# One-core attention and Strassen-type layer on Trainium2: running sums of phase one kept in PSUM, alpha folded into the weights, attention steps placed anew, early loads for phase two

## The chip, the cores and the metric

The kernel runs on one core of one Trainium2 chip. A core has TensorE (PE), VectorE (DVE), ScalarE (ACT), GpSimd (POOL) and SyncE (SP), which here only issues DMAs. The metric is the time of one execution on the device in microseconds. The kernel before has a median of 1134.48 us over 3 runs (1133.36 to 1135.65).

## The reference

All data are float32: 8 batches, 8 heads, 576 positions, head size 64; 4608 tokens of width 512; 2048 hidden features.

```python
k_p = k.reshape(B, H, 72, 8, D).mean(axis=3)      # v_p in the same way
scores = scale * q @ k_p.T;  scores -= max;  attn = exp(scores)
attn = attn / (attn.sum(-1) + 1e-09)
x = (attn @ v_p), heads side by side               # 4608 x 512
h = x @ w_in                                       # 4608 x 2048
g = h + sin(alpha * h)**2 / (alpha + 1e-09)        # alpha: one number per hidden feature
out = g @ w_out                                    # 4608 x 512
```

## The kernel before

**Tiling.** The tokens are cut into nine units of 512. Phase one makes x, h and g of unit after unit and stores g to a buffer in DRAM (`g_bridge`); phase two loads g and multiplies by `w_out`. Both matrix products are done by a Strassen-Winograd scheme: each factor is a 2 x 2 array of blocks, and seven block products with sums of blocks as operands take the place of eight.

**Phase one.** `hidden(u)` (L210 to L266) forms four sums of the blocks of x on VectorE (L210), then goes through four weight groups J = 0 to 3. A group is seven products of eight matmuls of 256 columns each (L222), in the order 1, 6, 7, 5, 2, 4, 3, into banks of the PSUM pool `ps_m` (five banks; the attention has three others, `ps_a`). Product 1 is copied to SBUF by ScalarE (`p1`), VectorE adds products 6 and 7 to it (`u2`, `u3`, L227 and the lines after it) and gets the four blocks of h from these sums; product 2 is added by the matmuls themselves onto the bank of product 1, and product 4 onto that of product 7. Then ScalarE takes four sines (L259) with alpha as the scale and one square over all 2048 columns (L260), VectorE adds the squares times 1/(alpha + 1e-9) to h (L264, four instructions), and SP stores the megabyte (L266).

**Attention.** `attention(b)` is a generator. One step is the transposes of pooled keys (L89), of queries, a score pair with its maximum (VectorE), the two exponentials of all tiles at once (L121), the norm of one tile (two VectorE operations and the reciprocal, then a multiply on POOL, L130), transposes of weights (L139), values (L153) or a rest. For batch 0 all steps run in the head, one after the other. While unit u computes, two steps of batch u + 1 are taken after each product, until they are used up. `load_batch` (L60 to L74) issues the loads of a batch and pools keys and values by eight on POOL (keys of batch 0 on VectorE).

**Weights.** `load_w_in` (L175 to L184) loads eight pieces of 512 KB on SP and forms three sums and differences per group and a fourth block, 16 instructions in all, on POOL (L179); ScalarE negates `a22`. `load_w_out` (L194, L195) is called at unit 7, after attention's pools have been closed: four loads of a megabyte into their memory, and four differences of 2048 elements on POOL.

**Phase two.** `output(u)` (L276 to L323) loads four megabytes of g in five buffers shared with the four sums per group that VectorE forms (`gs`, L279), and does seven products of 16 matmuls (L292) in the order 1, 6, 2, 7, 5, 4, 3. The pool of these buffers is opened only when the pools of phase one are closed.

**Order.** The instructions are written in one stream; a tile scheduler fixes each engine's order by its own estimate of times, adds the semaphores, and gives memory out. Each engine works through its queue in order, and so does SP with its DMAs.

In the program's names `a` are blocks of `w_in` and `as` sums of them, `b` and `bt` the same of `w_out` (`bt` also the sums of x), `ex` the exponentials, `ral` is 1/(alpha + 1e-9), `s` holds sines and squares.

## Time and profile before

| | |
|---|---|
| median of 3 runs | 1134.48 us |
| the profiled execution: its time, its span | 1131.5 us, 1129.7 us |
| mean granted TensorE clock over the span | 0.963 |
| PE, DVE, ACT, POOL busy | 92%, 50%, 26%, 22% of the span |
| head, first matmul of unit 0 | until 50.2 us |
| phase one ends, phase two starts | 670.8 us, 687.0 us |
| DMA over the span | 122.48 MB, mean 108 GB/s |

The span runs from the first to the last instruction that the hardware recorded. A group row gives line, engine, operation, output<-inputs, shape and count, then busy time and mean ns, then the idle time of the engine just ahead of these instructions and what ended most of it. A timeline row gives start and length in us, and in brackets the wait ahead of it and who ended it. A row of a stage gives start and end, length, busy time and count of each engine, the granted clock (1.00 is full), the share of the DMA engines and GB/s. A row of digits shows tenths in 40 equal slices. PE's busy time is modelled, so gaps between starts say more than it does.

### The profile page before, as it was taken

The numbers are of one execution on the slowest core, as the hardware profiler recorded it, in microseconds if no ns is written. First come the engines' busy times: TensorE is split into PE (matmuls) and PEld (weight loads), VectorE is DVE, ScalarE is ACT, GpSimd is POOL, SyncE is SP. The second block draws the span as 40 slices with busy tenths as digits, with TensorE's granted clock in tenths as the row PEclk, the third lists the DMA queues.
The fourth block names the chain that finished last, engine by engine and source line by source line (L and its number), as shares of the span: only waits on it lengthen the run. The fifth ranks groups of instructions, "written<-read, shape, count | busy, mean of one in ns | idle before, by whom it ended". The sixth has DMA issues, their size and how long they took to land. (4 is left out here: it accounts for less than half of the span.)

```text
span 1129.7 us, 13110 instructions
## 1 busy us (share of the span) xinstructions
PE 1041.6 (92%) x5248; PEld 880.1 (78%) x5248; DVE 565.4 (50%) x1019; ACT 296.2 (26%) x386; POOL 245.9 (22%) x248
## 2 busy tenths in 40 slices
PE   4579999989899899999949976999999999999998
PEld 3367777868778688888838865888888888888887
DVE  5548685785857667577674554033140413314030
ACT  2234444454443544445423540000000000000000
POOL 4997571350714502102060000000000000000000
PEclk9689999999999899999979997999999999999999
DMA  7363450612605214111242115134050432505120
GB/s 195 117 168 116 140 177 38 180 68 83 184 38 158 81 75 128 61 52 75 77 147 112 75 74 223 60 127 157 30 186 5 182 109 78 186 1 187 59 91 37
DMA packets 71212, 122.48 MB, mean 108 GB/s; under 512 B 41968, under 2 KB 46064, under 8 KB 61936
## 3 DMA queue, kind: packets, MB, share of 16 engines
q1 hardware_dynamic: 71152, 121.66, 31.7%
q8 instruction: 41, 0.67, 0.2%
q14 instruction: 19, 0.16, 0.0%
HBM read 74.46 MB, written 47.19 MB: 108 GB/s over the span
## 5 line engine op out<-in xcount | busy, mean ns | idle before, releaser
L222 PE MATMUL ps_m<-bt,a 128*128 128x256 f32 x576 | 143.6, 388 | 19.5 <-DVE u L227 19.5
L292 PE MATMUL ps_m<-b,g 128*128 128x256 f32 x576 | 131.0, 383 | 16.1 <-issue 16.1
L222 PE MATMUL ps_m<-bt,as 128*128 128x256 f32 x576 | 142.6, 387 | 0.0
L74 POOL TENSOR_TENSOR kvin<-kvin 72x512 f32<-72x512 f32 x120 | 129.9, 1085 | 51.2 <-DMA kvin<-in_v_dram 26.1
L222 PE MATMUL ps_m<-xT,a 128*128 128x256 f32 x576 | 140.8, 382 | 0.0
L222 PEld LDWEIGHTS ps_m<-bt,a 128*128 128x128 f32 x576 | 108.6, 194 | 34.9 <-DVE u L227 21.5
L292 PEld LDWEIGHTS ps_m<-b,g 128*128 128x128 f32 x576 | 110.2, 192 | 32.5 <-issue 16.4
L264 DVE SCALAR_TENSOR_TENSOR h<-s,ral,h 128x512 f32<-128x512 f32 x144 | 126.7, 937 | 7.8 <-ACT s L260 7.7
L292 PE MATMUL ps_m<-bt,gs 128*128 128x256 f32 x576 | 130.1, 381 | 0.0
L292 PE MATMUL ps_m<-b,gs 128*128 128x256 f32 x576 | 127.9, 379 | 0.0
L259 ACT ACTIVATE s<-h,al 128x512 f32<-128x512 f32 x144 | 96.5, 714 | 105.9 <-DVE h L227 105.9
L292 PEld LDWEIGHTS ps_m<-bt,gs 128*128 128x128 f32 x576 | 109.9, 191 | 15.4 <-issue 0.5
L227 DVE TENSOR_TENSOR h<-u,ps_m 128x512 f32<-128x512 f32 x108 | 73.7, 682 | 96.2 <-PE ps_m L222 94.6
L292 PEld LDWEIGHTS ps_m<-b,gs 128*128 128x128 f32 x576 | 109.4, 190 | 14.9
L222 PEld LDWEIGHTS ps_m<-bt,as 128*128 128x128 f32 x576 | 106.9, 191 | 17.6 <-issue 3.5
L222 PEld LDWEIGHTS ps_m<-xT,a 128*128 128x128 f32 x576 | 106.5, 190 | 16.8 <-issue 3.1
L303 ACT COPY p<-ps_m 128x512 f32<-128x512 f32 x9 | 5.3, 586 | 303.0 <-PE ps_m L292 303.0
L299 DVE TENSOR_TENSOR o<-u,ps_m 128x512 f32<-128x512 f32 x27 | 18.5, 686 | 118.2 <-PE ps_m L292 118.2
L279 DVE TENSOR_TENSOR gs<-g 128x512 f32<-128x512 f32 x72 | 47.1, 687 | 54.6 <-PE ps_m L292 29.0
L139 PE MATMUL ps_at<-ident,ex 128*72 128x128 f32 (+1 forms) x320 | 46.7, 295 | 26.0 <-POOL ex L130 26.0
L222 PE MATMUL ps_m<-xT,as 128*128 128x256 f32 x288 | 70.0, 386 | 0.0
L260 ACT ACTIVATE s<-s 128x2048 f32<-128x2048 f32 x36 | 68.8, 1910 | 0.4
(65 smaller groups left out, 1002.5 us busy)
## 6 DMA issues: line engine op xcount, KB each, us to landing
g_bridge<-h SPq DMA_DIRECT2D x36, 1024.0 KB
g<-g_bridge SPq DMA_DIRECT2D x36, 1024.0 KB
kvin<-in_k_dram SPq DMA_DIRECT2D x32, 288.0 KB
kvin<-in_v_dram SPq DMA_DIRECT2D x32, 288.0 KB
out_dram<-o SPq DMA_DIRECT2D x18, 512.0 KB
qm<-in_q_dram SPq DMA_DIRECT2D x32, 256.0 KB
a<-in_moe_w_in_dram SPq DMA_DIRECT2D x8, 512.0 KB
b<-in_moe_w_out_dram SPq DMA_DIRECT2D x4, 1024.0 KB
```

Of the source, the lines that this page charges most:

```text
L74: eng.tensor_tensor(out=o, in0=t[:, :, 0:w], in1=t[:, :, w:2 * w], op=OP.add)
L139: nc.tensor.transpose(ps[:, hh, :n], ex[:n, i, 4 * g + hh, :], self.ident[:n, :n])
L222: nc.tensor.matmul(bank[:, jj, :], self.A[p][:, kk, f * P:(f + 1) * P], Bx[p][:, kk, :], start=(first and jj == 0 and kk == 0), stop=(kk = ...
L227: add = lambda o, x, y: nc.vector.tensor_tensor(out=o, in0=x, in1=y, op=OP.add)
L259: nc.scalar.activation(out=s[:, i, :, jj, :], in_=h[:, i, :, jj, :], func=AF.Sin, scale=self.al[:, f:f + 1])
L260: nc.scalar.activation(out=s[:], in_=s[:], func=AF.Square)
L264: nc.vector.scalar_tensor_tensor(out=h[:, i, :, jj, :], in0=s[:, i, :, jj, :], scalar=self.ral[:, f:f + 1], in1=h[:, i, :, jj, :], op0=OP. ...
L279: tt = lambda o, x, y, op: nc.vector.tensor_tensor(out=o, in0=x, in1=y, op=op)
L292: nc.tensor.matmul(bank[:, t, :], G[J][p][:, jj, t * P:(t + 1) * P], self.Bw[p][:, J * JW + jj, :], start=(first and t == 0 and J == 0 and ...
L299: add = lambda o, x, y: nc.vector.tensor_tensor(out=o, in0=x, in1=y, op=OP.add)
L303: nc.scalar.copy(out=p1[:], in_=b1[:])
```

## The change

**Sums in PSUM.** The order of the products in a group is now 1, 5, 6, 2, 7, 3, 4. ScalarE copies product 1 from its bank into a second one (L320), and the matmuls of product 6 add to that copy; ScalarE copies the sum into a third bank (L328), and product 7 adds there. Product 2 adds onto the first bank, 3 onto the second, 4 onto the third. Only product 5 is copied to SBUF (`p5`, L324). VectorE adds p5 to two banks (L310), and the sines (L315, now eight of 256 columns a group) read PSUM directly where no p5 is needed. Matmuls that add to a bank need its words marked as written: at the start `mark_banks` writes each of the five banks with four matmuls of the identity (L283).

**Alpha in the weights.** `w_in` is multiplied by alpha + 1e-9, column by column, on VectorE (L245) from a broadcast copy of alpha (a megabyte in one of the buffers `h`), so that the banks hold (alpha + 1e-9) h; the sine has the scale `rat` = alpha/(alpha + 1e-9). Squares are added with plain adds, one of them of double width. In exchange `w_out`, whose rows are the hidden features, is multiplied by 1/(alpha + 1e-9) on ScalarE (L265, 32 instructions of 256 columns).

**Weight sums.** The sums of `w_in` (L242) go from POOL to VectorE, and are made group by group inside unit 0 (`combine_w_in`); the loads are 16 of 256 KB. The differences of `w_out` (L267) go from POOL to VectorE in four pieces each, within the steps of unit 7.

**Attention.** The 27 steps between products of a unit share 48 steps of the next batch evenly. A tile's norm is issued a step ahead of the transposes of the tile before it, and two steps after the exponentials are empty. For batch 0 there is one exponential per tile.

**Phase two.** A pool `gp` of four buffers on the right side, opened at unit 7 with the memory of attention, takes the loads of phase two's unit 0 ahead of the closing of phase one. Loads of a unit are issued at the end of the unit before. The products go in the order 1, 4, 2, 6, 7, 5, 3; product 4 has a bank of its own and is copied to SBUF.

The diff, cut to its core:

```diff
+        def exp_one(i):
+            n = tiles[i][1]
+            nc.scalar.activation(out=ex[:n, i], in_=ex[:n, i], func=AF.Exp, scale=scale)
...
+        yield k_t()
+        for hp in range(NP):
+            yield q_t(hp)
+        yield q_rest()
+        for i in range(5):
...
+                yield score(i, g)
+            if b == 0:
+                exp_one(i)
+        if b:
+            yield exp()
+            yield
+            yield
+        eng = nc.gpsimd
...
+        yield norm(0, eng)
+        yield norm(1, eng)
+        yield a_t(0, 0)
+        yield a_t(0, 1)
+        for c in range(2):
+            yield norm(2 * c + 2, eng)
+            yield a_t(2 * c + 1, 0)
+            yield a_t(2 * c + 1, 1)
+            if c == 0:
+                yield norm(3, eng)
+                for hp in range(NP):
+                    yield values(0, hp)
+                yield a_t(2, 0)
+                yield a_t(2, 1)
+        for hp in range(NP):
+            yield values(1, hp)
+        yield a_t(4, 0)
+        yield a_t(4, 1)
+        for hp in range(NP):
+            yield values(2, hp)
...
+    def load_alpha(self):
+        nc = self.nc
+        self.al = self.const.tile([P, self.K2], F32, name="al")
+        self.ral = self.const.tile([P, self.K2], F32, name="ral")
+        self.rat = self.const.tile([P, self.K2], F32, name="rat")
+        self.alb = self.hp.tile([P, self.FF], F32, name="h")
+        with nc.allow_non_contiguous_dma(reason="2048 words once"):
+            nc.sync.dma_start(out=self.al[:], in_=self.alpha.rearrange("(k p) -> p k", p=P))
+        nc.sync.dma_start(out=self.alb[:], in_=self.alpha.partition_broadcast(P))
+        nc.vector.tensor_scalar(out=self.ral[:], in0=self.al[:], scalar1=1e-9, scalar2=None, op0=OP.add)
+        nc.vector.reciprocal(out=self.ral[:], in_=self.ral[:])
+        nc.vector.tensor_tensor(out=self.rat[:], in0=self.al[:], in1=self.ral[:], op=OP.mult)
+        nc.vector.tensor_scalar(out=self.alb[:], in0=self.alb[:], scalar1=1e-9, scalar2=None, op0=OP.add)
...
-        c = h // 2
-        for x in range(2):
-            for t, j, i in ((a21, 0, 1), (a22, 1, 1), (a11, 0, 0), (a12, 1, 0)):
-                nc.sync.dma_start(out=t[:, :, x * c:(x + 1) * c], in_=src[:, 2 * j:2 * j + 2, i * h + x * c:i * h + (x + 1) * c])
...
+            for t, j, i in ((a21, 0, 1), (a22, 1, 1), (a11, 0, 0), (a12, 1, 0)):
+                nc.sync.dma_start(out=t[:, :, s], in_=src[:, 2 * j:2 * j + 2, i * h + J * w:i * h + (J + 1) * w])
+
+    def combine_w_in(self, J):
+        s = slice(J * w, (J + 1) * w)
+        tt = lambda o, x, y, op: nc.vector.tensor_tensor(out=o[:, :, s], in0=x[:, :, s], in1=y[:, :, s], op=op)
+        for t, i in ((a21, 1), (a22, 1), (a11, 0), (a12, 0)):
+            c = self.alb[:, i * h + J * w:i * h + (J + 1) * w]
+            nc.vector.tensor_tensor(out=t[:, :, s], in0=t[:, :, s], in1=c.unsqueeze(1).to_broadcast([P, 2, w]), op=OP.mult)
+        tt(s1, a21, a22, OP.add)
+        tt(s2, s1, a11, OP.subtract)
+        tt(a21, a11, a21, OP.subtract)
+        tt(s4, a12, s2, OP.subtract)
+        nc.scalar.mul(out=a22[:, :, s], in_=a22[:, :, s], mul=-1.0)
...
-        tt = lambda o, x, y: nc.gpsimd.tensor_tensor(out=o[:], in0=x[:], in1=y[:], op=OP.subtract)
-        tt(t1, b12, b11)
-        tt(t2, b22, t1)
...
+        for c in range(0, kk, 2):
+            for t, i in ((b11, 0), (b12, 0), (b22, 1), (b21, 1)):
+                for k in range(c, c + 2):
+                    f = i * kk + k
+                    nc.scalar.mul(out=t[:, k], in_=t[:, k], mul=self.ral[:, f:f + 1])
+            s = slice(c, c + 2)
+            tt = lambda o, x, y: nc.vector.tensor_tensor(out=o[:, s], in0=x[:, s], in1=y[:, s], op=OP.subtract)
+            tt(t1, b12, b11)
+            tt(t2, b22, t1)
+            tt(b12, b22, b12)
+
+            tt(t4, b21, t2)
+            yield
...
+    def mark_banks(self):
+
+        nc = self.nc
+        for _ in range(5):
+            ps = self.ps_m.tile([P, 4, P], F32, name="ps_m", tag="m")
+            for j in range(4):
+                nc.tensor.matmul(ps[:, j, :], self.ident[:], self.ident[:], start=(j == 0), stop=(j == 3), skip_group_check=True)
...
+        def group(J):
+            if first:
+                self.combine_w_in(J)
...
+            def sin(i, j, src):
...
+                    nc.scalar.activation(out=s[:, i, j, jj, :], in_=src[:, jj, :], func=AF.Sin, scale=self.rat[:, f:f + 1])
+
+            b1, b5 = bank(), bank()
+            product(1, J, b1, True)
+            b6 = bank()
+            nc.scalar.copy(out=b6[:], in_=b1[:])
+            yield
+            product(5, J, b5, True)
+            p5 = self.tp.tile([P, JW, TH], F32, name="p5")
+            nc.scalar.copy(out=p5[:], in_=b5[:])
+            yield
+            product(6, J, b6, False)
+            b7 = bank()
+            nc.scalar.copy(out=b7[:], in_=b6[:])
+            yield
+            product(2, J, b1, False)
+            sin(0, 0, b1)
+            yield
+            product(7, J, b7, False)
+            add(g[:, 1, 1], b7[:], p5[:])
+            sin(1, 1, g[:, 1, 1])
+            nc.scalar.activation(out=s[:, 0, 0], in_=s[:, 0, 0], func=AF.Square)
+            add(g[:, 0, 0], b1[:], s[:, 0, 0])
+            yield
+            product(3, J, b6, False)
+            add(g[:, 0, 1], b6[:], p5[:])
+            sin(0, 1, g[:, 0, 1])
+            yield
+            product(4, J, b7, False)
+            sin(1, 0, b7)
+            nc.scalar.activation(out=s[:, 0, 1], in_=s[:, 0, 1], func=AF.Square)
+            nc.scalar.activation(out=s[:, 1], in_=s[:, 1], func=AF.Square)
+            add(g[:, 1, 0], b7[:], s[:, 1, 0])
+            add(g[:, :, 1], g[:, :, 1], s[:, :, 1])
+            nc.sync.dma_start(out=self.gd[u, J], in_=g[:].rearrange("p a b c d -> p (a b c d)"))
+            yield
...
-            b1 = bank()
-            product(1, b1, True)
-            p1 = tmp("p1")
-            nc.scalar.copy(out=p1[:], in_=b1[:])
-            yield
-            b6 = bank()
-            product(6, b6, True)
-            u2 = tmp("u2")
-            add(u2[:], p1[:], b6[:])
...
-            nc.scalar.activation(out=s[:], in_=s[:], func=AF.Square)
-            for i in range(2):
-                for jj in range(JW):
-                    f = i * self.K2 // 2 + J * JW + jj
-                    nc.vector.scalar_tensor_tensor(out=h[:, i, :, jj, :], in0=s[:, i, :, jj, :], scalar=self.ral[:, f:f + 1],
-                                                   in1=h[:, i, :, jj, :], op0=OP.mult, op1=OP.add)
...
+    def load_g(self, u):
+        g = []
+        for J in range(self.NJ):
+            t = self.gp.tile([P, 2, 2, JW, TH], F32, name="g")
+            self.nc.sync.dma_start(out=t[:].rearrange("p a b c d -> p (a b c d)"), in_=self.gd[u, J])
+            g.append(t)
+        return g
...
+        b4 = bank()
+        product(4, b4)
+        p4 = tmp("p4")
+        nc.scalar.copy(out=p4[:], in_=b4[:])
+        product(2, b1, False)
+        nc.scalar.copy(out=C(1, 1), in_=b1[:])
         b6 = bank()
-        product(6, b6, True)
+        product(6, b6)
...
+                self.mark_banks()
...
-                    if u == self.B - 1:
+                        steps = 48
+                    elif u == self.B - 1:
                         att.close()
                         wo = pool(top, "wo", 1, side="right")
-                        self.load_w_out(wo)
-                    for _ in self.hidden(u):
-                        next(nxt, None)
-                        next(nxt, None)
+                        self.gp = pool(top, "gp", self.NJ, side="right")
+                        nxt = self.load_w_out(wo)
+                        steps = 14
+                    n = done = 0
+                    for _ in self.hidden(u, u == 0):
+                        n += 1
+                        while done < n * steps // 27:
+                            next(nxt, None)
+                            done += 1
                     for _ in nxt:
                         pass
-            self.gp = pool(top, "gp", 5)
+                g = self.load_g(0)
+            self.gs = pool(top, "gs", self.NJ)
             self.op = pool(top, "op", 2)
             for u in range(self.NU):
-                self.output(u)
+                self.output(u, g)
+                if u + 1 < self.NU:
+                    g = self.load_g(u + 1)
```

Three places where this moves instructions. First, POOL's queue in the head, from the last pooled values of batch 0 on (`a` and `as` are the blocks and sums of `w_in`, `ex` and `sm` exponentials and norms). Before:

```order
L74 TENSOR_TENSOR vp<-kvin 72x128
L179 TENSOR_TENSOR as_154<-a_152,a_153 128x2x256 x2
L179 TENSOR_TENSOR as_155<-as_154,a_150 128x2x256
L179 TENSOR_TENSOR a_152<-a_150,a_152 128x2x256
L179 TENSOR_TENSOR as_155<-as_154,a_150 128x2x256
L179 TENSOR_TENSOR a_152<-a_150,a_152 128x2x256
L179 TENSOR_TENSOR as_156<-a_151,as_155 128x2x256 x2
L130 TENSOR_TENSOR ex<-ex,sm 128x576 x3
```

After:

```order
L78 TENSOR_TENSOR vp<-kvin 72x128
L144 TENSOR_TENSOR ex<-ex,sm 128x576 x4
L144 TENSOR_TENSOR ex<-ex,sm 64x576
L78 TENSOR_TENSOR kvin<-kvin 72x2x256
L78 TENSOR_TENSOR kvin<-kvin 72x2x128
L78 TENSOR_TENSOR kp<-kvin 72x128
```

The weight sums are gone from POOL; the softmax multiplies (L130, now L144) follow the pooled values at once, and batch 1's keys come behind the five multiplies.

Second, the preparation of `w_out` in unit 7. Before, on POOL (b_4009, 4010, 4012 and 4011 are b11, b12, b22 and b21):

```order
L195 TENSOR_TENSOR bt_4013<-b_4010,b_4009 128x2048
L195 TENSOR_TENSOR bt_4014<-b_4012,bt_4013 128x2048
L195 TENSOR_TENSOR b_4010<-b_4012,b_4010 128x2048
L195 TENSOR_TENSOR bt_4015<-b_4011,bt_4014 128x2048
```

After, a stretch of ScalarE's queue in unit 7, the first and second group (b_4118, 4119, 4121 and 4120 are b11, b12, b22 and b21; L320 copies product 1 into the bank of product 6):

```order
L320 COPY ps_m<-ps_m 128x512
L324 COPY p_4116<-ps_m 128x512
L328 COPY ps_m<-ps_m 128x512
L265 ACTIVATE b_4118<-b_4118,ral 128x256 x2
...
L315 ACTIVATE s<-ps_m,rat 128x256
L265 ACTIVATE b_4119<-b_4119,ral 128x256 x6
L315 ACTIVATE s<-ps_m,rat 128x256
L345 ACTIVATE s<-s 128x512
L265 ACTIVATE b_4121<-b_4121,ral 128x256 x6
L346 ACTIVATE s<-s 128x1024
L265 ACTIVATE b_4120<-b_4120,ral 128x256 x6
L320 COPY ps_m<-ps_m 128x512
```

The work on `w_out` has left POOL, and ScalarE now has 26 scalings ahead of the second group's first copy.

Third, SP's queue at the border of the phases. Before:

```order
L266 DMA g_bridge<-h 128x2048 x7
L194 DMA b_4009<-in_moe_w_out_dram 128x8x256
L266 DMA g_bridge<-h 128x2048
L194 DMA b_4010<-in_moe_w_out_dram 128x8x256
L194 DMA b_4012<-in_moe_w_out_dram 128x8x256
L194 DMA b_4011<-in_moe_w_out_dram 128x8x256
L266 DMA g_bridge<-h 128x2048 x8
L276 DMA g<-g_bridge 128x2048 x7
L323 DMA out_dram<-o 128x2x512
```

After:

```order
L349 DMA g_bridge<-h 128x2048
L259 DMA b_4119<-in_moe_w_out_dram 128x8x256
L259 DMA b_4121<-in_moe_w_out_dram 128x8x256
L259 DMA b_4120<-in_moe_w_out_dram 128x8x256
L361 DMA g<-g_bridge 128x2048 x3
L349 DMA g_bridge<-h 128x2048
L361 DMA g<-g_bridge 128x2048
L349 DMA g_bridge<-h 128x2048 x7
L361 DMA g<-g_bridge 128x2048 x4
L418 DMA out_dram<-o 128x2x512 x2
```

Four loads of g for phase two now stand among and ahead of the last eight stores of phase one; before, all of them stood behind the last store.

229 lines of the change are left out of this document (93 added, 136 removed).

## The prediction

> **What bounds the kernel now.** I read the page first, then the span by stages, then the waits. "Unit" is one of the nine 512-token pieces of phase one (units 0 to 8), "product" one of the seven of a weight group, eight TensorE records.
>
> ```profile
> PE 1041.6 (92%) x5248; PEld 880.1 (78%) x5248; DVE 565.4 (50%) x1019; ACT 296.2 (26%) x386; POOL 245.9 (22%) x248
> PEclk9689999999999899999979997999999999999999
> ```
>
> TensorE does nearly all of it, so only its gaps, and the slow clock around them, can be won. The stages (start to end, length, busy PE, PEld, DVE, ACT, POOL, then the granted clock): head; unit 0; units 1 to 4; 5 and 6; 7; 8; the border between the phases; phase two.
>
> ```profile
> 0.00:50.20 50.20, 22.71 (x113) 16.50 (x114) 24.98 (x58) 11.14 (x16) 35.17 (x40) 0.76 0.60 173
> 50.20:132.60 82.40, 73.11 (x390) 58.43 (x390) 51.10 (x94) 30.86 (x40) 65.39 (x73) 0.94 0.49 139
> 132.60:415.60 283.00, 269.02 (x1473) 221.14 (x1472) 197.10 (x382) 129.11 (x166) 110.20 (x116) 0.98 0.35 110
> 415.60:549.50 133.90, 132.87 (x753) 110.30 (x752) 93.63 (x196) 65.03 (x85) 16.01 (x16) 1.00 0.20 75
> 549.50:622.30 72.80, 56.92 (x285) 47.27 (x285) 48.60 (x57) 23.47 (x33) 19.14 (x4) 0.88 0.32 116
> 622.30:670.80 48.50, 48.50 (x225) 42.30 (x224) 25.97 (x39) 22.24 (x30) 0.00 (x0) 1.00 0.21 87
> 670.80:687.00 16.20, 0.15 (x2) 0.07 (x1) 3.68 (x6) 3.78 (x4) 0.00 (x0) 0.62 0.39 158
> 687.00:1130.00 443.00, 438.32 (x2016) 384.14 (x2016) 120.35 (x189) 10.55 (x18) 0.00 (x0) 0.99 0.28 104
> ```
>
> Units 5 and 6 take 66.95 us each with almost no gap, units 1 to 4 70.75. Unit 8, without attention, takes 48.5; its floor comes from two product starts 1.73 us apart (timeline of TensorE):
>
> ```profile
> 188.40 1.89 PE L222 MATMUL ps_m<-xT,as 128*128 128x256 f32 x8
> 190.13 1.89 PE L222 MATMUL ps_m<-xT,a 128*128 128x256 f32 x8
> ```
>
> 28 products are 48.4 us, and phase two's 2016 records at 0.216 are 435 of its 443. So phase two has nothing to give but its first unit's cold start. The gaps that TensorE does have, as the list of waits names them (total, times, longest):
>
> ```profile
> PE ps_at L139 <- POOL ex L130: 26.0, 8, 12.2
> PE ps_m L222 <- DVE u L227: 19.5, 5, 15.9
> PE ps_m L292 <- issue: 16.1, 1, 16.1
> ```
>
> **The head and unit 0.** In the head the transposes of the weights of attention wait for POOL, which does the first weight sums (L179) before the softmax multiplies (L130):
>
> ```profile
> 10.59 0.38 PE L89 MATMUL ps_kt<-ident,kp 72*128 72x72 f32 x1 [1.79 <-DVE kp L74]
> 19.03 6.32 SPq L175 DMA_DIRECT2D a<-in_moe_w_in_dram  x8
> 26.40 2.49 POOL L179 TENSOR_TENSOR as<-a,a 128x512 f32<-128x512 f32 x2 [0.53 <-DMA a<-in_moe_w_in_dram]
> 36.18 3.36 POOL L130 TENSOR_TENSOR ex<-ex,sm 128x576 f32<-128x576 f32 x3
> 37.38 3.63 PE L139 MATMUL ps_at<-ident,ex 128*72 128x128 f32 x16 [12.18 <-POOL ex L130]
> 56.59 1.21 DVE L210 TENSOR_TENSOR bt<-bt,xT 128x512 f32<-128x512 f32 x1
> 63.63 2.77 PE L222 MATMUL ps_m<-bt,as 128*128 128x256 f32 x6
> ```
>
> The change gives POOL the multiplies at once (front part) and VectorE the sums. VectorE adds 1e-9 to the broadcast alpha before the last scores; that megabyte can be there about when the first megabyte of weights is now (26.4). The add has no row: 2048 elements lie between one 512-wide operation (0.7) and four (2.9); I take 2. Then two reductions, a scale and a reciprocal (about 2.3) and one multiply (3.36 / 3 = 1.1): the transposes start near 33 instead of 37.4. From there the old kernel needed 20.4 us to its last input sum (57.8). The new one has VectorE alone in the way; four weight scalings and the first sum are added, POOL no longer delays the multiplies: 20.5 again, so continuous products from about 53.5, with two products done against one and a quarter at 63.6. That is 10.1 + 1.3 = 11.4 us.
>
> Two things there I cost at nothing. The 20 marking matmuls are 40 records of 128 columns at half of 0.216: 4.3 us, 8.6 at half clock. They are over before the last pooled keys come at 10.59; without that cover they cost their own length. And SP issues 16 weight loads where the row has 8 in 6.3 us, so batch 1's keys go out some 6 us later, near 32; POOL wants them only after its five multiplies, near 38. Beyond that, each microsecond late would hold the key transposes, which stand in TensorE's queue among the first products.
>
> Unit 0 then pays. Its VectorE work:
>
> ```profile
> L264 DVE SCALAR_TENSOR_TENSOR h<-s,ral,h 128x512 f32<-128x512 f32 x12 | 13.1, 1149 | 0.5 <-ACT s L260 0.5
> L264 DVE SCALAR_TENSOR_TENSOR h<-s,ral,h 128x512 f32<-128x512 f32 x16 | 11.1, 744 | 0.4 <-ACT s L260 0.4
> L227 DVE TENSOR_TENSOR u<-p,ps_m 128x512 f32<-128x512 f32 x36 | 24.6, 683 | 49.0 <-PE ps_m L222 48.8
> L210 DVE TENSOR_TENSOR bt<-xT 128x512 f32<-128x512 f32 x18 | 13.1, 737 | 0.0
> ```
>
> Units 5 and 6 show 46.8 us of VectorE each, unit 8 26.0 without attention, so attention and input sums are about 21. The new group has four adds of 0.683 and one of double width (0.68 to 1.37; 1.2): 3.9 us where five adds and four L264 were 6.4. Four groups: 15.7. The remaining 28 scalings and sums of weights at 0.69 are 19.3. Together 56. The first two rows are L264 in unit 0 (66 to 126 us, POOL nearly always at work) and in unit 6 (POOL idle): two SBUF operands cost 1149 against 744 ns. At +0.4 for 32 such operations VectorE has 69. TensorE has 66.95 - 3.5 = 63.5 left (a unit less two products). VectorE's queue is in order and waits for TensorE at its start and end, so neither the 56 nor the 63.5 will do; I take 68, just under the 69 that the contended row gives. Unit 0 ends at 121.5 instead of 132.6: **11 us** won. Bounds: 15.5 (TensorE alone decides), 2 (69 and 8 more of mutual waiting).
>
> The Trainium skill ("SBUF — State Buffer", Who interferes with whom) says that a VectorE instruction with two SBUF inputs and a GpSimd instruction that reads SBUF lock each other out for the whole instruction. The two L264 rows agree. Read at its hardest, it speaks against moving the sums, and makes the rival "lock" below.
>
> **Units 1 to 6.** Two empty steps after the exponentials and multiplies issued a step ahead leave POOL time; of the 26.0 us, 12.2 were in the head, and the rest goes, with the slow clock behind it (0.98). In exchange TensorE now waits inside a group for copies on ScalarE: product 1, copy into a second bank, product 6, copy, product 7.
>
> ```profile
> L259 ACT ACTIVATE s<-h,al 128x512 f32<-128x512 f32 x144 | 96.5, 714 | 105.9 <-DVE h L227 105.9
> L260 ACT ACTIVATE s<-s 128x2048 f32<-128x2048 f32 x36 | 68.8, 1910 | 0.4
> L231 ACT COPY p<-ps_m 128x512 f32<-128x512 f32 x36 | 20.4, 568 | 3.0 <-PE ps_m L222 2.7
> L121 ACT ACTIVATE ex<-ex 128x2304 f32<-128x2304 f32 x8 | 17.0, 2127 | 8.1 <-DVE ex L117 8.0
> L121 ACT ACT_TABLE_LOAD x7 | 9.0, 1283 | 0.1
> ```
>
> L260 and L121 differ by 256 columns and 217 ns, so a half-width sine is 0.50, a 512 square 0.61, a 1024 square 1.04. A group has three copies (1.7), eight sines (4.0) and squares (2.3): 8.0 us, against 4 of L259, one L260 and two copies, 5.9. Four times 8.0 plus attention's share (32.5 a unit in units 5 and 6, less 4 x 5.9, about 9) is 41 of 67: it fits. The tight link is from product 4 to the next group's product 6: two sines, a square and a copy (2.6) against products 1 and 5 (3.5). Where the exponentials stand, two copies, a table load and the long exponential (0.57 + 1.28 + 2.13 + 0.57 = 4.6) run against products 6 and 2, a quarter of the next product 1 and the last scores, 3.9 and a little: even. So I cost the links at half a microsecond a unit: 67.5 instead of 70.75 and 66.95. 416.9 - 405 = **12 us**. Bounds: 66.9 each (+15.5), and 0.7 us late in every group (70.3: -5). A copy into PSUM has no row; I take that into SBUF, and the lateness bound covers it.
>
> **Unit 7.** Today POOL forms the w_out sums, and VectorE stands:
>
> ```profile
> 559.84 0.38 SPq L194 DMA_DIRECT2D b<-in_moe_w_out_dram  x1
> 572.60 4.52 POOL L195 TENSOR_TENSOR bt<-b,b 128x2048 f32<-128x2048 f32 x1 [46.29 <-DMA b<-in_moe_w_out_dram]
> 572.98 19.39 DVE L264 SCALAR_TENSOR_TENSOR h<-s,ral,h 128x512 f32<-128x512 f32 x4 [0.22 <-ACT s L260]
> 593.02 3.58 PE L222 MATMUL ps_m<-bt,a 128*128 128x256 f32 x8 [15.88 <-DVE u L227]
> DMA  0000049899999999999000000000000000991000
> ```
>
> That goes. But the 32 new scalings stand in ScalarE's queue, behind loads issued when attention's last copies free the memory (front part): the copy that lets product 6 of the second group start stands behind 26 of them. The last row (555 to 600 us in 40 slices) shows those loads busy from 560.6 to about 576.5, so the fourth block lands 17 us after the first issue, the second 12.8 (572.6). From the issue: products 5 and 6 and a copy, 4.5; the first block, say 6; then 26 scalings and 8 sines at 0.45 (back to back), squares and copy (2.9), no further wait for blocks as each lands before its turn: 24.2. TensorE gets there after eight products, 13.8. So **the stall returns on ScalarE**: 10.4 us, and 1.5 of slow clock, instead of 15.9 and about 1.5. With 0.5 for the later scalings: **4 us** won. VectorE's 16 differences of these blocks wait for the same scalings, and behind them stand the last adds and the store of unit 7's first group; nobody on TensorE needs those before its third group. Bounds: all blocks 6 us later (-3), scalings at 0.35 and early blocks (+9).
>
> **The border.**
>
> ```profile
> 675.04 2.74 DVE L264 SCALAR_TENSOR_TENSOR h<-s,ral,h 128x512 f32<-128x512 f32 x4 [3.40 <-ACT s L260]
> 681.75 2.50 SPq L276 DMA_DIRECT2D g<-g_bridge  x5
> 686.96 2.05 PE L292 MATMUL ps_m<-b,g 128*128 128x256 f32 x4 [16.05 <-issue]
> ```
>
> The loads for phase two wait for the last store because they need its memory. In the change the loads of unit 0 stand on SP before the last eight stores, in a pool of their own, and products 1, 4 and 2 read loaded tiles alone: 48 matmuls, 20.7 us, in which VectorE forms the 16 differences (16 x 0.69 = 11) and the last store lands. So 16.2 goes, and most of the first unit's cold start (443 - 435 less ordinary small gaps), 1.3: **17.5 us**. Bounds 14 to 18.5.
>
> **Sum.** 11 + 12 + 4 + 17.5 = 44.5. The profiled execution took 1131.5 us (span 1129.7 and 1.8 around it); it becomes 1087. The median of the runs shown is 3.0 above it: **1090 us**.
>
> **The rivals.** *Full cover* (17%): every term at its upper bound, 15.5 + 15.5 + 9 + 18.5 = 58.5: 1076. For it: VectorE has room in units 1 to 6. *Lock* (9%): every one of the 32 two-SBUF operations of unit 0 waits out a POOL operation of about 1.1 us: 56 + 35 = 91, unit 0 ends at 144.5, 23 later than forecast: 1113. Against it: L264 lost only 0.4 at the busiest. *Links late* (13%): 0.7 us in each of 36 groups, 25: 1115. *Early loads not early* (3%): the border stays, 1107. *Slower* (6%): the same links, but at over 1.25 us a group (44.5 / 36) they eat everything; at 1.6, 1148. It decides if ScalarE's in-order queue holds a copy behind one sine pair and one wait per link. Against it: 41 of 67 us of work, and unit 8's measured 22.2 of 48.5 leaves room. *Forecast* 52%.
>
> A difference under 0.2% cannot be told from none in this kernel. Faster 92%, same 2%, slower 6%. The range 1069 to 1114 holds the forecast, full cover, lock and the border case.
>
> **What would show it.** POOL no longer ahead of the first L154 transposes, which start near 33; unit 0 with VectorE near 60 busy of 68; units 1 to 6 at 67 to 68; one TensorE wait of about 10 us on ScalarE early in unit 7; no gap at the border. Wrong if units 1 to 6 exceed 70, if many short TensorE waits name L320 or L328, or if the gap of unit 7 is gone.

## The result and the profile after

The changed kernel takes 1082.5 us (median; 1079.9 to 1084.5) against 1134.9 in the same session: a ratio of 0.954 (95% interval 0.951 to 0.956), 52 us less. Forecast were 1090 and a range of 1069 to 1114. The profiled execution took 1081.1 us with a span of 1079.3, 50.4 less than before. The first page of its profile:

```profile
PE 1037.8 (96%) x5288; PEld 879.6 (81%) x5288; DVE 494.9 (46%) x925; ACT 376.6 (35%) x682; POOL 218.1 (20%) x228
PEclk9799999999999999999989999999999999999999
```

TensorE is 96% busy instead of 92%, VectorE has 70 us less and ScalarE 80 us more. The stages, cut at the same events as in the prediction (start to end, length, busy PE, PEld, DVE, ACT, POOL, granted clock, DMA share, GB/s): head; unit 0; units 1 to 6; unit 7; unit 8; phase two, which now follows without a border.

```profile
0.00:42.90 42.90, 28.86 (x152) 23.11 (x153) 27.29 (x64) 9.35 (x15) 18.45 (x25) 0.80 0.87 223
42.90:125.00 82.10, 72.53 (x419) 56.37 (x418) 68.54 (x119) 41.88 (x74) 73.38 (x69) 1.00 0.53 134
125.00:523.80 398.80, 396.40 (x2218) 328.80 (x2217) 231.32 (x479) 236.31 (x419) 126.26 (x135) 1.00 0.34 105
523.80:588.80 65.00, 54.56 (x265) 45.35 (x264) 30.49 (x50) 41.35 (x89) 0.00 (x0) 0.92 0.53 194
588.80:637.20 48.40, 48.40 (x226) 42.72 (x226) 17.72 (x24) 29.39 (x57) 0.00 (x0) 1.00 0.21 88
637.20:1079.30 442.10, 437.01 (x2017) 383.28 (x2015) 119.54 (x191) 18.30 (x32) 0.00 (x0) 1.00 0.25 100
```

Against the stages before, head and unit 0 together are 132.6 - 125.0 = 7.6 us shorter, units 1 to 6 416.9 - 398.8 = 18.1, unit 7 72.8 - 65.0 = 7.8, unit 8 0.1, and border with phase two (1129.7 - 670.8) - 442.1 = 16.8. The sum is 50.4. What TensorE still waits for, the four largest (total, times, longest):

```profile
PE ps_m L302 <- ACT ps_m L320: 10.3, 1, 10.3
PE ps_at L154 <- POOL ex L144: 8.0, 3, 5.1
PE ps_sc L123 <- DVE ex L127: 5.9, 6, 2.9
PE ps_kt L102 <- POOL kp L78: 5.0, 3, 2.0
```

The 26 us for POOL's multiplies are 8.0, of which 5.1 are in the head. The waits for `u` and at the border are gone. New is one wait of 10.3 us for a ScalarE copy.

### The profile page after: what moved, and what is told of

Read it like the earlier page. It is cut to its first block, busy times and chain, and to the rows that moved or that the text cites. A ratio compares the mean times of both kernels' runs of the same rounds, so it can differ in the third digit from the quotient of the medians.

```text
span 1079.3 us, 13285 instructions
## 1 busy us (share of the span) xinstructions
PE 1037.8 (96%) x5288; PEld 879.6 (81%) x5288; DVE 494.9 (46%) x925; ACT 376.6 (35%) x682; POOL 218.1 (20%) x228
## 4 chain that ended last, share of the span: by engine, by line
PE 84%; POOL 6%; DMA 4%; ACT 2%; DVE 2%; SPq 1%; issue 1%; POOLq 0%; ACTq 0%
PE ps_m L384 40%; PE ps_m L302 34%; POOL kvin L78 4%; PE ps_sc L123 3%; PE ps_o L164 3%; PE ps_at L154 2%; DMA kvin<-in_v_dram 1%; DMA a<-in_moe_w_in_dram 1%; DMA kvin<-in_k_dram 1%; ACT b L265 1%; SPq L64 1%; PE ps_qt L109 1%; DMA b<-in_moe_w_out_dram 1%; POOL vp L78 1%; POOL kp L78 1%
## 5 line engine op out<-in xcount | busy, mean ns | idle before, releaser
L302 PE MATMUL ps_m<-bt,as 128*128 128x256 f32 x576 | 138.7, 388 | 10.4 <-ACT ps_m L320 10.3
L78 POOL TENSOR_TENSOR kvin<-kvin 72x512 f32<-72x512 f32 x120 | 132.9, 1110 | 55.2 <-DMA kvin<-in_v_dram 33.2
L302 PE MATMUL ps_m<-bt,a 128*128 128x256 f32 x576 | 139.6, 381 | 0.0
L384 PE MATMUL ps_m<-bt,gs 128*128 128x256 f32 x576 | 127.3, 380 | 0.0
L384 PEld LDWEIGHTS ps_m<-bt,gs 128*128 128x128 f32 x576 | 109.8, 191 | 14.5
L384 PEld LDWEIGHTS ps_m<-b,g 128*128 128x128 f32 x576 | 109.8, 191 | 14.5
L302 PEld LDWEIGHTS ps_m<-xT,a 128*128 128x128 f32 x576 | 106.5, 191 | 18.1 <-issue 4.6
L310 DVE TENSOR_TENSOR h<-ps_m,s 128x512 f32<-128x512 f32 x72 | 49.5, 687 | 122.0 <-ACT s L336 80.8
L315 ACT ACTIVATE s<-h,rat 128x256 f32<-128x256 f32 x144 | 65.6, 500 | 64.0 <-DVE h L310 63.9
L391 DVE TENSOR_TENSOR u<-p,ps_m 128x512 f32<-128x512 f32 x9 | 6.2, 688 | 169.0 <-PE ps_m L384 152.8
L315 ACT ACTIVATE s<-ps_m,rat 128x256 f32<-128x256 f32 x144 | 60.2, 467 | 40.8 <-PE ps_m L302 40.2
L144 POOL TENSOR_TENSOR ex<-ex,sm 128x576 f32<-128x576 f32 (+1 forms) x40 | 47.9, 1223 | 98.1 <-DVE sm L142 98.1
L384 PE MATMUL ps_m<-bt,g 128*128 128x256 f32 x288 | 63.6, 380 | 0.0
```

Source lines behind the costliest of these rows:

```text
L78: eng.tensor_tensor(out=o, in0=t[:, :, 0:w], in1=t[:, :, w:2 * w], op=OP.add)
L144: eng.tensor_tensor(out=ex[:n, i], in0=ex[:n, i], in1=sm[:n].unsqueeze(2).to_broadcast([n, H, Sp]), op=OP.mult)
L302: nc.tensor.matmul(ps[:, jj, :], self.A[p][:, kk, f * P:(f + 1) * P], Bx[p][:, kk, :], start=(start and jj == 0 and kk == 0), stop=(kk == ...
L310: add = lambda o, x, y: nc.vector.tensor_tensor(out=o, in0=x, in1=y, op=OP.add)
L315: nc.scalar.activation(out=s[:, i, j, jj, :], in_=src[:, jj, :], func=AF.Sin, scale=self.rat[:, f:f + 1])
L384: nc.tensor.matmul(ps[:, t, :], G[J][p][:, jj, t * P:(t + 1) * P], self.Bw[p][:, J * JW + jj, :], start=(start and t == 0 and J == 0 and j ...
```

## The experiments

### Unit 7: how many scalings stand ahead of the copy

In the changed kernel ScalarE and TensorE show this around the new wait (start, length; an excerpt of ScalarE's timeline, and then TensorE's):

```profile
538.30 0.91 ACT L265 ACTIVATE b<-b,ral 128x256 f32<-128x256 f32 x2 [3.95 <-DMA b<-in_moe_w_out_dram]
...
544.68 2.50 ACT L265 ACTIVATE b<-b,ral 128x256 f32<-128x256 f32 x6
547.08 0.47 ACT L315 ACTIVATE s<-ps_m,rat 128x256 f32<-128x256 f32 x1
547.43 0.63 ACT L345 ACTIVATE s<-s 128x512 f32<-128x512 f32 x1
547.95 2.50 ACT L265 ACTIVATE b<-b,ral 128x256 f32<-128x256 f32 x6
550.35 1.05 ACT L346 ACTIVATE s<-s 128x1024 f32<-128x1024 f32 x1
551.29 2.50 ACT L265 ACTIVATE b<-b,ral 128x256 f32<-128x256 f32 x6
553.68 0.59 ACT L320 COPY ps_m<-ps_m 128x512 f32<-128x512 f32 x1
```

```profile
542.02 2.00 PE L302 MATMUL ps_m<-bt,as 128*128 128x256 f32 x8
554.33 2.08 PE L302 MATMUL ps_m<-bt,as 128*128 128x256 f32 x4 [10.31 <-ACT ps_m L320]
```

From the landing of the first block on, ScalarE waits for no further block: it is busy without a pause until the copy. Two kernels change how many scalings stand ahead. In the first, `load_w_out` yields once after its four loads, and the run hands its steps out in unit 8; the scheduler pulls them forward again, but only the first eight stand ahead of the copy.

```diff
-                        nxt = self.load_w_out(wo)
+                        late = self.load_w_out(wo)
+                        next(late)
+                    else:
+                        nxt = late
                         steps = 14
```

> The changed kernel, with the steps on w_out handed out in unit 8 instead of unit 7; the scheduler pulls them forward, but only 8 scalings (those of b11) now stand ahead of the copy that product 6 of unit 7's second group waits for, where the changed kernel has 26. Theory (ScalarE's queue in order): in the changed kernel b11 landed at 538.3 us and the copy ran at 553.7, 15.4 us later, 10.4 of it scalings at 0.40 and 5.0 sines and squares; with 8 scalings it runs 3.2 + 5.2 = 8.4 after the landing, TensorE is dry at 543.9, and the wait falls from 10.3 to about 3: 1075. Rival (the wait is for the landing of the blocks themselves, which are no earlier): the wait stays near 10 and the time at 1082.

The second also takes the factor from a copy that VectorE writes in the second group of unit 7, so that no scaling can start before that:

```diff
+            if u == self.B - 1 and J == 1:
+                nc.vector.scalar_tensor_tensor(out=self.ral2[:], in0=g[:, 0, 0, 0, 0:self.K2], scalar=0.0, in1=self.ral[:], op0=OP.mult, op1=OP.add)
...
-                    nc.scalar.mul(out=t[:, k], in_=t[:, k], mul=self.ral[:, f:f + 1])
+                    nc.scalar.mul(out=t[:, k], in_=t[:, k], mul=self.ral2[:, f:f + 1])
```

> The same, and the scalings take their factor from a copy of ral that VectorE writes in the second group of unit 7 (one operation of 16 elements), so that none can stand ahead of the second group's copies; they spread over the rest of units 7 and 8. Theory: no wait of TensorE on L320's copy in unit 7, 10.3 us and about 1 of slow clock gone: 1071. Rival (the work, not its place, is what costs): the 13 us of scalings crowd ScalarE in unit 8 (29 busy of 48 there now), TensorE waits for copies in many short pieces, and the time stays above 1077.

They took 1071.7 us (1070.6 to 1076.5) and 1072.0 (1070.8 to 1072.8), both 11 below the change. In TensorE's list of waits the first has for unit 7

```profile
PE ps_m L303 <- DVE h L311: 1.6, 1, 1.6
```

and the second has left of all waits for that copy, in the whole span,

```profile
PE ps_m L304 <- ACT ps_m L322: 0.8, 2, 0.4
```

Unit 7 took 55.7 and 54.2 us instead of 65.0. So the wait was the place of the scalings in ScalarE's queue, with the landing of the first block inside it, and not the amount of work: in the second kernel the same 32 scalings, spread over the rest of units 7 and 8, cost nothing that TensorE waits for. In the first a remnant is left. ScalarE stands 2.2 us at its first scaling until the block lands (535.3), a square behind it comes late, VectorE's `h` waits for that square until 537.5, and TensorE waits 1.6 us for `h`. The remnant is below the 3 us expected, since the block landed 12.7 us after the start of unit 7, where it took 14.5 in the changed kernel (538.3 - 523.8).

### Units 1 to 6: the attention steps, the sums in PSUM, and both

Two kernels complete a table of two parts of the change: the new attention steps, and the new sums, which here stand for all that the change does inside a group, alpha in the weights included. One is the changed kernel with the old order of attention for batches 1 to 7 (two steps a product, the norm directly ahead of its transposes, no empty steps):

```diff
-            yield
-            yield
...
-        yield norm(0, eng)
-        yield norm(1, eng)
...
+            for i in range(5):
+                yield norm(i, eng)
+                yield a_t(i, 0)
+                yield a_t(i, 1)
...
-                        steps = 48
+                        steps = 54
```

> The changed kernel, with the attention of batches 1 to 7 in the steps of the kernel before: two steps after each product, each tile's norm right before its transposes, no empty steps. Theory A (units 1 to 6 gained because VectorE and POOL have less beside them, whatever the order of steps): units 1 to 6 stay at 66.5 us each, time 1083. Theory B (they gained because the norms stand ahead): TensorE waits on the softmax multiplies come back, 14 us in the kernel before outside the head, with the clock behind them about 18: 1100.

The other is the kernel before with the new order alone:

```diff
+        yield
+        yield
+        yield norm(0)
+        yield norm(1)
+        yield a_t(0, 0)
...
-                        next(nxt, None)
-                        next(nxt, None)
+                        n += 1
+                        while done < n * 48 // 27:
+                            next(nxt, None)
+                            done += 1
```

> The kernel before, with the change's attention steps alone (48 steps over the 27 gaps of a unit, norms a step ahead of the transposes before them, two empty steps after the exponentials) for batches 1 to 7; batch 0 as before. Theory A (the PSUM sums made units 1 to 6 shorter): they stay at 69.5 us on average, time 1133. Theory B (the steps did): units 1 to 6 fall to about 66.5, 18 us less: 1117.

They took 1112.8 us (1109.7 to 1113.8) and 1122.4 (1121.4 to 1122.7). Units 1 to 6 of the kernel before, of the old sums with the new steps, and of the new sums with the old steps, with the waits of TensorE in that stretch under each:

```profile
132.60:549.50 416.90, 401.89 (x2225) 331.44 (x2224) 290.73 (x578) 194.14 (x250) 126.21 (x132) 0.98 0.30 99
PE ps_at L139 <- POOL ex L130: 13.3, 6, 4.9
```

```profile
131.10:540.40 409.30, 401.09 (x2226) 327.14 (x2225) 287.76 (x578) 193.75 (x251) 125.70 (x132) 1.00 0.31 101
PE ps_sc L113 <- DVE ex L117: 4.2, 4, 1.1
PE ps_at L142 <- POOL ex L132: 2.1, 4, 0.8
PE ps_o L152 <- ACT aT L144: 1.9, 2, 1.0
```

```profile
128.20:550.60 422.40, 404.08 (x2217) 331.51 (x2216) 230.45 (x479) 237.09 (x419) 123.45 (x133) 0.98 0.32 97
PE ps_at L154 <- POOL ex L144: 15.4, 6, 4.5
PE ps_m L309 <- ACT ps_m L327: 2.9, 6, 0.5
```

| units 1 to 6, us | old attention steps | new attention steps |
|---|---|---|
| sums on VectorE | 416.9 | 409.3 |
| sums in PSUM | 422.4 | 398.8 |

Neither theory holds by itself. The new steps alone win 7.6 us: six waits for POOL's multiplies, one a batch, shrink from 13.3 to 2.1, and the slow clock behind them goes; but waits for VectorE and for ScalarE's copies, 4.2 and 1.9, come up, and VectorE is as busy as before (288 us). The new sums alone lose 5.5: VectorE has 60 us less, yet TensorE waits on POOL as long as before, and six times, once a batch, for the bank copy (0.5 each). Together they win 18.1, 16 more than the sum of the two. Of the 10.5 us between 409.3 and 398.8 the named waits account for 5.8 (8.2 against 1.9 and 0.5 in the change); the other 4.7 stand in the rows as busy time of TensorE (401.1 against 396.4), and what stretched it was not traced.

What of the new steps matters was tried on the changed kernel, first without the two empty steps:

```diff
             yield exp()
-            yield
-            yield
```

> The changed kernel without the two empty steps after the exponentials (norms still a step ahead, 48 steps). Theory (the empty steps give ScalarE and POOL the time they need, 0.57 + 1.28 + 2.13 + 0.57 us of exponentials and then a norm and a multiply of 1.1): TensorE waits about 2 us for the first multiply of every batch, 14 in all: 1096. Rival (the norms ahead do it): within 3 us of 1082.5.

and then with each norm directly ahead of its own transposes again, the empty steps and the 48 steps kept:

```diff
+            for i in range(5):
+                yield norm(i, eng)
+                yield a_t(i, 0)
+                yield a_t(i, 1)
```

> The changed kernel with the empty steps and the 48 steps, but each norm right before its own transposes again for batches 1 to 7. All three undone together cost 30 us (1112.8). Theory (the norms ahead are the larger part, since each of five multiplies a batch takes 1.1 us and more on POOL while TensorE has half a product, 0.9 us): 1100. Rival (the empty steps and the even spacing are): under 1090.

They took 1087.4 us (1085.1 to 1088.8) and 1086.4 (1083.9 to 1087.2): 5 and 4 more than the change, where the theories had 14 and 18. All three parts undone cost 30. Units 1 to 6 took 402.9 and 402.6 us, and TensorE waited there for POOL's multiplies once a batch, 3.5 and 4.6 us in all, against 15.4 with all three parts undone. So neither part alone carries the gain. Two readings are left: empty steps and norms ahead cover for each other, or the even spacing, which both kernels keep, does most of it. How much of the remaining 21 us is the spacing, and how much the pair together, no run separates.

### The links between the products

In this kernel both copies from bank to bank are done twice.

```diff
             nc.scalar.copy(out=b6[:], in_=b1[:])
+            nc.scalar.copy(out=b6[:], in_=b1[:])
...
             nc.scalar.copy(out=b7[:], in_=b6[:])
+            nc.scalar.copy(out=b7[:], in_=b6[:])
```

> The changed kernel, with both copies from bank to bank done twice (0.57 us each, 72 more copies). It measures the slack of the links that I costed at half a microsecond a unit. If the links have no slack, 72 x 0.57 = 41 us: 1124. If each has more than 0.6 us, nothing but ScalarE's place in unit 7 (1 us): 1084. What the prediction said (tight but nearly even, half a microsecond late in a unit) lies near the first: over 1105.

It took 1094.2 us (1091.0 to 1098.8), 12 more; 41 more was the price without slack. The profile is of the longest of its executions; 7.0 us of what it has more lie before the end of unit 0. Units 1 to 6 took 407.2, 8.4 more for 48 further copies (ScalarE is busy 24 us longer). TensorE's largest wait there:

```profile
PE ps_m L302 <- ACT ps_m L321: 4.1, 6, 1.4
```

Six waits in 24 groups: one a unit. ScalarE's timeline shows which (the last of them):

```profile
499.70 2.12 ACT L131 ACTIVATE ex<-ex 128x2304 f32<-128x2304 f32 x1
...
511.43 0.60 ACT L320 COPY ps_m<-ps_m 128x512 f32<-128x512 f32 x1
511.94 1.06 ACT L348 ACTIVATE s<-s 128x1024 f32<-128x1024 f32 x1
512.89 0.59 ACT L321 COPY ps_m<-ps_m 128x512 f32<-128x512 f32 x1
```

It is the first link of the group after the exponentials. ScalarE had stood 1.7 us for VectorE's `h` until 507.95, is busy without a pause from there on, and a square stands between the two copies. The prediction had called this link tight, with 2.6 us against 3.5; the links inside the group of the exponentials, which it had called even, hold. So this link has less than half a microsecond of slack, and no other link shows in the list. Of the 8.4 us, 4.5 are busy time of TensorE (400.9 against 396.4) that no row places. The copies themselves cost what was taken from the copy into SBUF:

```profile
L324 ACT COPY p<-ps_m 128x512 f32<-128x512 f32 x36 | 21.1, 585 | 49.4 <-PE ps_m L302 49.4
L320 ACT COPY ps_m<-ps_m 128x512 f32<-128x512 f32 x36 | 20.7, 575 | 17.7 <-PE ps_m L302 17.7
L328 ACT COPY ps_m<-ps_m 128x512 f32<-128x512 f32 x36 | 20.6, 572 | 38.9 <-PE ps_m L302 38.9
```

### The head and unit 0

Three kernels ask what bounds unit 0. The first issues the loads of batch 1's keys between the two halves of the loads of `w_in`:

```diff
-                self.load_w_in()
+                self.load_w_in((0, 1))
+                one_ = self.load_batch(1)
+                next(one_)
+                self.load_w_in((2, 3))
```

> The changed kernel, with the four loads of batch 1's keys issued after the first eight of the sixteen loads of w_in instead of after all sixteen. In the changed kernel SP issues them at 35.1 us, POOL gets them at 42.95 after 4.3 us idle, and TensorE waits 5.0 us in three pieces for the pooled keys. Theory (the step that I costed at nothing costs these 5 us): the loads go out near 29, POOL goes on at 38.6, TensorE no longer waits for pooled keys; 4 us and some clock: 1078. Rival (VectorE bounds unit 0 anyway, its sums of the first group end at 56.5 and then bind): the wait moves to VectorE, under 1 us won: 1082.

The second moves the sums of `w_in` back to POOL, in their new place:

```diff
-        tt = lambda o, x, y, op: nc.vector.tensor_tensor(out=o[:, :, s], in0=x[:, :, s], in1=y[:, :, s], op=op)
+        tt = lambda o, x, y, op: nc.gpsimd.tensor_tensor(out=o[:, :, s], in0=x[:, :, s], in1=y[:, :, s], op=op)
```

> The changed kernel, with the sums of w_in (L242, 16 operations) on POOL again but in their new place, group by group in unit 0; the multiplies by alpha stay on VectorE. Theory (VectorE bounds unit 0): VectorE loses 16 operations of about 1.1 us, 18 us, of which some 5 come off the end of unit 0: 1078. Rival (POOL bounds it: 73 of 82 us are busy there in unit 0): keys and sums queue on POOL, unit 0 grows by the 16 x 1.25 = 20 us: 1100.

The third leaves out the multiplies of `w_in`:

```diff
-            nc.vector.tensor_tensor(out=t[:, :, s], in0=t[:, :, s], in1=c.unsqueeze(1).to_broadcast([P, 2, w]), op=OP.mult)
```

> The changed kernel without the 16 multiplies of w_in by alpha + 1e-9 on VectorE (this part of the computation is left out; alpha is loaded and used elsewhere as before). They are 16 us of VectorE's 68.5 in unit 0. Theory (VectorE bounds unit 0, as predicted): unit 0 ends some 8 us earlier than 125.0: 1074. Rival (POOL's chain of pooled keys, values and multiplies bounds it, 73 of 82 us busy): unit 0 ends within 2 us of where it did: 1081 or 1082.

They took 1077.7 us (1076.6 to 1079.9), 1092.4 (1090.9 to 1094.2) and 1076.7 (1074.6 to 1078.0). The stage of unit 0 with the sums on POOL, and without the multiplies:

```profile
42.00:141.20 99.20, 79.28 (x419) 61.41 (x418) 54.31 (x103) 40.87 (x73) 87.52 (x86) 0.89 0.46 118
```

```profile
43.40:124.20 80.80, 72.82 (x418) 56.28 (x417) 58.57 (x103) 41.36 (x73) 67.90 (x72) 1.00 0.58 144
```

With 14 us less on VectorE and 14 more on POOL, unit 0 ends 16 us later, and TensorE waits 9.8 us at once for a multiply of POOL (0.9 in the change). The multiplies of `w_in` are 10 us of VectorE there, not the 16 of the expectation. Without them POOL is busy 5.5 us less too; unit 0 ends 0.8 us earlier (3.6 at most against the kernels that are alike up to there), unit 1 3.4 earlier, and the whole takes 5.8 us less, which lies between the two expectations. VectorE's load has a share in these two units, but unit 0 does not end when VectorE is done. Nor does POOL alone set its length: TensorE itself is busy for 72.5 of the 82.1 us, and its waits there are 5.0 us for POOL's pooled keys, 2.9 for scores on VectorE, 0.9 for a multiply of POOL and 0.7 for a copy of ScalarE. What starts POOL's pooled keys late shows in the changed kernel's queues: SP, then POOL, around the issue of batch 1's keys.

```profile
20.48 2.55 SPq L219 DMA_DIRECT2D h<-in_moe_alpha_dram  x1
23.07 11.61 SPq L236 DMA_DIRECT2D a<-in_moe_w_in_dram  x16
35.12 11.54 SPq L70 DMA_DIRECT2D kvin<-in_k_dram  x4
```

```profile
31.53 7.08 POOL L144 TENSOR_TENSOR ex<-ex,sm 128x576 f32<-128x576 f32 x5 [4.21 <-DVE sm L142]
42.95 2.45 POOL L78 TENSOR_TENSOR kvin<-kvin 72x512 f32<-72x512 f32 x2 [4.34 <-DMA kvin<-in_k_dram]
```

With the keys between the halves POOL begins on them at 37.2 instead of 42.95, ahead of its last multiply, unit 0 ends at 123.1, and TensorE's wait for pooled keys falls from 5.0 to

```profile
PE ps_kt L103 <- POOL kp L78: 2.5, 1, 2.5
```

The median is 4.8 us lower. That interval (0.949 to 0.953 of the kernel before) overlaps the change's; the pair of kernels at the end repeats the difference.

### The border

The pool of phase two's loads is opened only after phase one's are closed:

```diff
-                        self.gp = pool(top, "gp", self.NJ, side="right")
...
-                g = self.load_g(0)
+            self.gp = pool(top, "gp", self.NJ)
+            g = self.load_g(0)
```

> The changed kernel, with the pool of phase two's loads opened after phase one is closed, so that they wait for its last store again. Forecast of the prediction: the border is worth 17.5 us (14 to 18.5), so 1100 (1096 to 1101), with a gap of about 16 us between the phases. Rival (the order of products 1, 4, 2 does part of it, since three products need no sums): the gap is there but the cold start behind it is shorter, 1097.

It took 1091.9 us (1087.1 to 1094.2), 9.4 more and not 17.5. Its gap between the phases is

```profile
645.13 2.05 PE L384 MATMUL ps_m<-b,g 128*128 128x256 f32 x4 [5.09 <-DMA g<-g_bridge]
```

and its first unit of phase two takes 52.6 us instead of 48.5. Two things besides the early loads made the old border longer. SP's queue here, and VectorE's last work of phase one:

```profile
640.07 0.80 SPq L361 DMA_DIRECT2D g<-g_bridge  x2
644.34 0.32 SPq L349 DMA_DIRECT2D g_bridge<-h  x1
```

```profile
643.10 1.22 DVE L310 TENSOR_TENSOR h<-h,s 128x1024 f32<-128x1024 f32 x1
```

The first two loads go out at 640.07, as the last matmuls of phase one end, 4.3 us ahead of the last store, where in the kernel before all five loads stood behind it, at 681.75. And the last block of h is ready 4.3 us after phase one's last matmul (640.0), where four L264 ended 6.9 us after it (677.8 against 670.9). So of the 16.8 us that border and phase two lost, 9 hang on the early pool; the other 7 came with the shorter end of a group, the new places of the buffers and the new order of the products, which no run separates.

### Both repairs

The scalings held back and the keys between the halves, in one kernel:

> The changed kernel with both repairs: the scalings of w_out held back behind the second group of unit 7, and the loads of batch 1's keys between the two halves of the loads of w_in. Alone they gave 1072.0 and 1077.7 against 1082.5. Theory (two waits at different places, so they add): 1082.5 - 10.5 - 4.8 = 1067. Rival (the keys' gain was the spread between runs of a head full of DMAs, unit 0 ending between 123.1 and 127.8 us in kernels that are alike up to there): 1071 to 1072.

It took 1066.8 us (1065.8 to 1067.4), 0.940 of the kernel before (0.938 to 0.943) and 5.2 less than the scalings held back alone, whose lowest time lies 3.3 above the highest here. The two add, as expected. It is the fastest version here, 16 us below the change. TensorE's largest waits in it:

```profile
PE ps_at L155 <- POOL ex L145: 5.4, 2, 5.0
PE ps_sc L124 <- DVE ex L128: 5.2, 8, 1.8
PE ps_kt L103 <- POOL kp L78: 3.9, 2, 3.0
```

All are in the head and around units 0 and 1.

## Why the prediction was right, point by point

**What bounds the kernel.** That only TensorE's gaps could be won held: unit 8 stayed at 48.4 us, and phase two ran at 48.5 a unit, 0.2 above what it was.

**The head.** The transposes began at 32.7 (forecast near 33), and two products were done at 53.9 (53.5). The first is closer than its terms, which sum to 31.8: the addition to alpha began at 27.57 and not at 26.4, and took 1.23 and not 2. The marking matmuls ended at 9.5, with the last pooled keys at 11.2, and cost nothing. The second thing costed at nothing failed: I counted eight more weight loads on SP, 6 us, but not the 2.55 us of the alpha broadcast, and not that the keys then land only 8 us after they are issued. POOL had them at 42.95 and not by 38, and TensorE waited 5.0 us. That is enough for the 3.4 us by which head and unit 0, with 7.6, fell short of 11; the kernel with the keys between, 4.8 faster, speaks for it.

**Unit 0.** That the unit ends with VectorE was wrong, by the two kernels that relieve it and by VectorE's own load. The 68.5 us of its row count from 42.9; from 53.5, where the forecast starts, VectorE was busy for 58.2 of 71.5 us, near the "60 busy of 68" among the signs and not the 56 + 32 x 0.4 of the sum. TensorE was busy for 64.9 of them, for which the forecast had 63.5, and waited in the rest. So the term of 68 was the load of the wrong engine, and that it lay only 3.5 us off was luck. The contention itself came out near the estimate from L264. The sums s1 of `w_in`, of the first three groups and of the fourth, and two like instructions of POOL at the time of the fourth:

```profile
L242 DVE TENSOR_TENSOR as<-a,a x3: 672/1208/1747, 50.0 to 81.8; 128x512 f32<-128x512 f32 x3
L242 DVE TENSOR_TENSOR as<-a,a x1: 675/675/675, 99.5 to 99.5; 128x512 f32<-128x512 f32 x1
```

```profile
98.15 2.39 POOL L78 TENSOR_TENSOR vp<-kvin 72x128 f32<-72x128 f32 x1
...
104.71 0.45 POOL L78 TENSOR_TENSOR vp<-kvin 72x128 f32<-72x128 f32 x1
```

The sums take from 0.67 to 1.75 us, 1.02 on average over all 16 (16.3 us). In the fourth group VectorE ran at its shortest, and it was POOL that waited: an addition of 0.45 us took 2.39, across three such operations of VectorE in a row (98.34 to 100.22). The Trainium skill ("SBUF — State Buffer", Who interferes with whom) has VectorE's operations with two SBUF inputs contend with GpSimd's reads, and the order of issue decide who blocks. The rows agree on the contention; the order they do not bear out, since POOL's addition is recorded 0.2 us ahead of the first of the three (spans on POOL are rough). The rival "lock" fell because each of the 16 lost 0.35 us on average, not the 1.1 of a whole pooling addition. The price has a second half, on POOL, that I had not costed: without the multiplies POOL was busy 5.5 us less.

**Units 1 to 6.** The mechanism (time for POOL) was right, the size was not: 12 forecast with a bound of 15.5, 18.1 measured. The failed step is "half a microsecond a unit" for the links, and the bound taken from units 5 and 6. TensorE names no link wait in these units. And the bound took six full units: units 5 and 6 hold 376.5 TensorE records each, units 1 to 6 of the change 2218 (before: 2225) and not 2259, because the last batch's attention runs on into unit 7. For each record the two took the same, 0.178 and 0.180 us. I also took the reordered steps and the PSUM sums for two separate gains; the table shows that they need each other.

**Unit 7.** The wait came back on ScalarE as forecast: 10.31 us for 10.4, TensorE dry 14.1 us after the first load's issue (529.8) for 13.8, and the copy done 24.5 after it for 24.2. The 24.2 is partly luck, since two of its terms were off and nearly cancelled: the first block landed 8.5 us after its issue and not 6, and from there to the end of the copy it took 16.0 us and not 18.2, with the scalings 0.40 apart. The unit won 7.8 us and not 4. The prediction's own terms give 5.0 (15.9 + 1.5 - 10.4 - 1.5 - 0.5), and the two stalls differ by 5.6; the rest goes with 20 fewer attention records in the unit (265 records against 285) and a better clock (0.92 against 0.88).

**The border.** Forecast 17.5, measured 16.8. The gap is gone, 16.2, and the first unit's cold start was 2.4 us; the ordinary units then gave 1.7 back. The price is right, but not all of it belongs to the early loads.

**Sum.** 11 + 12 + 4 + 17.5 = 44.5 against 7.6 + 18.1 + 7.8 + 0.1 + 16.8 = 50.4. The main error, units 1 to 6, was in the direction of the rival "full cover"; the two rivals that hung on late links fell.

## What to carry to other kernels

When work that waits for a load is handed to an engine whose queue runs in order, look at what stands behind it: 32 cheap scalings cost nothing or 11 us, by their place alone, and a scheduler will pull them forward unless their data hold them back. Price each moved part both alone and with the others undone: here two parts that win 8 and lose 5 alone win 18 together. And count every DMA that a queue issues ahead of the one that matters, with its landing, not only the new ones of its kind.

## What was not expected

Doing the bank copies twice showed that the tightest link is not in the group of the exponentials but the first of the next group, where ScalarE is late (TensorE waits 1.4 us at most); the prediction's figures left it 0.9 us to spare. The copy from bank to bank took the same time as the one into SBUF (0.57 and 0.59 us). And the ends of unit 0 in kernels that are alike up to there spread from 125.0 to 127.8 us, so that a change of one or two microseconds in that stage can't be read from one profile.
